# Reordering the first loads of a two-layer transformer kernel: one Wq quarter later, the second group's layernorm and transposes earlier, biases first on POOL

## Chip, cores, metric

The kernel runs on one core of one Trainium2 chip. The metric is device time in microseconds (us) of that core. Lower is better. Engines: PE (TensorE, matmul), VectorE (DVE in the profile), ScalarE (ACT), POOL (GpSimd), SP (SyncE, which here only issues DMA).

## The reference

One sequence of 2048 tokens of width 1024, in bfloat16, goes twice through two blocks: dilated local attention (32 heads, each position attends to 8 earlier positions, 2 apart) and a GELU feed-forward of width 3584.

```python
def _A_ref(x, wqkv, wo):                      # attention
    qkv = (x @ wqkv) ...                      # q, k, v: 32 heads of 32
    idx = pos[:, None] - arange(8) * 2        # masked where negative
    logits = einsum("bhsd,bhswd->bhsw", q, k[idx]) * scale
    o = einsum("bhsw,bhswd->bhsd", softmax(logits), v[idx])
    return o @ wo
x = x + _A_ref(_layernorm(x), A_wqkv, A_wo)
x = x + _B_ref(_layernorm(x), w1, b1, w2, b2)   # _B_ref: gelu(x @ w1 + b1) @ w2 + b2
# ... and both once more
```

## The kernel before

The tokens are cut into four groups of 512, four x tiles of 128 tokens each: tiles 0 to 3 are group 0, 4 to 7 group 1, 8 to 11 group 2, 12 to 15 group 3. Almost everything told here happens in the first 75 us, most of it in the stage that computes Q, K and V of group 0. Four parts matter.

The first loads, all on SP's queue:

```python
load_x(0, 0, 2)                          # x tiles 0, 1
wq_first = [load_qkv_half(0, 0, 2)]      # first half of Wq, as two quarters of 512 KB
load_x(0, 2, 4)                          # x tiles 2, 3
wq_first.append(load_qkv_half(0, 1, 2))  # second half
```

The layernorm of a tile: statistics on VectorE, the reciprocal root on POOL (two tiny operations), the normalisation on VectorE, and then a transpose, which is a DMA issued by SP for every group but the first.

```python
vec.bn_stats(...)            # twice per tile
vec.bn_aggr(mv, stats)
pool.tensor_tensor(rstd, mv[:, 1:2], eps_t, op=add)
pool.tensor_tensor(rstd, rstd, mhalf, op=pow)
vec.tensor_scalar(out=xn, in0=x[t], scalar1=mv[:, 0:1], scalar2=rstd, ...)
sp.dma_start_transpose(xnT[:, tt, :, :], xn ...)      # group 0 goes through PE instead
```

The logits, as products on VectorE (one per chunk of four channels, with an add tree over four chunks) that PE then sums over heads. A *head sum* needs four products and three adds:

```python
def new_prod(n, c):          # called after K chunk c has been copied out of PSUM
    vec.tensor_tensor(out=prod, in0=q chunk, in1=8 shifted views of the k chunk, op=mult)
    ...                      # tree: three adds per four products
def head_sum(n, last=True):  # eight matmuls on PE
    mm(L[...], lhsT=smat, rhs=prod ...)
```

And the program of the stage. PE runs its 24 chunks (8 of Q, 8 of K, 8 of V, each 8 matmuls of 128x512) in program order; `at(u, f)` calls `f` after chunk `u`. The order within VectorE, SP and ScalarE is chosen by a scheduler when the program is built; POOL keeps program order.

```python
build_constants()                         # POOL: halo zeros, masks ...
load_x(1)
stage(gen_qkv(0, 2), sides=at(0, ln_a, 1)         # layernorm of group 1 (tiles 4 to 7)
      + at(1, load_x, 3) + at(6, ln_a, 2, early)  # layernorm of group 2 (tiles 8 to 11)
      + at(14, load_bias)                         # bias load on POOL, then its transpose on PE
      + at(19, head_sum, 0, False))               # first head sum
q1 = gen_qkv(1, ...)
stage(q1, sides=at(5, attend, 0) + ...)           # attend(0): second head sum, softmax
```

Inside `gen_qkv(0)`: `load_x(2)` (tiles 8 to 11) and Wv are issued before the layernorm of group 1.

## Time and profile before

| | before |
|---|---|
| time, median of 3 runs (first measurement) | 1247.19 us (1247.05 to 1248.7) |
| span of the profiled run | 1245.8 us, granted PE clock 0.998 |
| PE busy | 1232.6 us, 99% |

From the page of the kernel before: busy time by engine, and the shares of the chain of waits that ended last.

```profile
...
PE 1232.6 (99%) x5821; PEld 633.5 (51%) x5871; DVE 835.9 (67%) x864; ACT 306.2 (25%) x477; POOL 99.1 (8%) x215
...
PE 96%; DMA 2%; DVE 1%; POOL 1%; issue 0%; SPq 0%; DVEq 0%
...
```

PE is the bound, and a share of 99% looks as if there were nothing to win. But a busy PE need not be PE at full speed: from 44 to 46 us (below) PE counts as busy for all of 2.00 us at a granted clock of 0.50, with 6 matmuls, where the same 2.00 us from 48 to 50 us hold 11 at 1.00. So we look at PE's waits. This is the wait list of PE over the whole execution (engine and line, what it waited for, us in total, number of waits, longest):

```profile
...
PE acc L179 <- DMA abc<-in_B_b_dram: 3.6, 1, 3.6
PE L L210 <- ACT xnT L93: 1.8, 1, 1.8
...
PE acc L118 <- ACT xnT L93: 0.9, 2, 0.7
```

Line L93 is the helper that issues all VectorE, ScalarE, POOL and SP instructions and L118 the one of PE's matmuls, so one reads the tile names: `acc` are PSUM accumulators, `L` the tile of the head sums (and, early on, of two transposes), `abc` first holds the biases. PE waits 3.6 us for the bias load, and 1.8 + 0.9 us in the first 18 us for copies of transposed tiles.

The wait for the biases costs more than 3.6 us. Stretches of 2 us of PE (columns: stretch; total; PE busy and number of matmuls; granted clock; share of the DMA engines; GB/s):

```profile
...
core 0: us, PE busy (x), PEclk, DMA share, GB/s
...
42.00:44.00 2.00, 1.27 (x5) 0.83 1.24 326
44.00:46.00 2.00, 2.00 (x6) 0.50 0.90 282
46.00:48.00 2.00, 2.00 (x9) 0.82 1.13 293
...
```

Behind the wait the granted clock is 0.50, and the trace has nine matmuls 427 ns apart where the others are 216 ns apart. From 46.75 us on PE has no more gap until the end.

The timeline of the stage (start, duration, engine, operation, count, and in brackets the idle time before it and what ended it). `big<-qT,kT` are products, `big<-big` adds, `L<-big,smat` is a head sum, `xn<-x` a normalisation, `rstd` POOL's part of a layernorm:

```profile
...
31.65 2.24 DVE L93 TENSOR_TENSOR big<-qT,kT 128x4096 bf16<-128x4096 bf16 x1
...
37.51 0.74 POOL L93 DMA_DIRECT2D abc<-in_B_b_dram  x1
...
42.06 0.55 DVE L93 TENSOR_SCALAR xn<-x,mv,rstd 128x1024 bf16<-128x1024 bf16 x1 [2.70 <-DMA xnT<-xn]
...
42.73 0.18 PE L179 MATMUL acc<-ident,abc 28*128 28x28 bf16 x1 [3.64 <-DMA abc<-in_B_b_dram]
...
42.85 10.54 PE L118 MATMUL acc<-xnT,wt 128*128 128x512 bf16 x40
...
47.04 4.62 DVE L93 TENSOR_TENSOR big<-big 128x4096 bf16<-128x4096 bf16 x2
...
53.32 0.61 PE L118 MATMUL L<-big,smat 128*32 128x512 bf16 x8
...
53.87 17.49 PE L118 MATMUL acc<-xnT,wt 128*128 128x512 bf16 x80
...
71.28 0.61 PE L118 MATMUL L<-big,smat 128*32 128x512 bf16 x8
...
```

Read it so. The first product starts at 31.65 us. The biases go out on POOL at 37.51, because POOL keeps program order and the last `rstd` of tiles 8 to 11 is ahead of them; they land at 42.69. PE then runs to the first head sum at 53.32. VectorE's last add before the first head sum ends at 47.04 + 4.62 = 51.66, so that sum has 1.7 us of slack and PE does not wait.

The wait for a copy in the first 18 us, in ScalarE's timeline: the copy of tile 2's transposes (`xnT<-L`) stands behind two copies of halo zeros, which wait for a POOL memset (`zhalo`) that is issued behind tile 3's `rstd`.

```profile
...
15.01 0.28 ACT L93 COPY kT<-zhalo 128x112 bf16<-128x112 bf16 x1 [5.16 <-POOL zhalo L93]
...
15.39 1.00 ACT L93 COPY xnT<-L 128x1024 bf16<-128x1024 bf16 x1
...
```

### The profile page before, as it was taken

The numbers are of one execution on the slowest core, as the hardware profiler recorded it, in microseconds if no ns is written. First come the engines' busy times: TensorE is split into PE (matmuls) and PEld (weight loads), VectorE is DVE, ScalarE is ACT, GpSimd is POOL, SyncE is SP. The second block draws the span as 40 slices with busy tenths as digits, with TensorE's granted clock in tenths as the row PEclk, the third lists the DMA queues.
The fourth block names the chain that finished last, engine by engine and source line by source line (L and its number), as shares of the span: only waits on it lengthen the run. The fifth ranks groups of instructions, "written<-read, shape, count | busy, mean of one in ns | idle before, by whom it ended". The sixth has DMA issues, their size and how long they took to land.

```text
span 1245.8 us, 14060 instructions
## 1 busy us (share of the span) xinstructions
PE 1232.6 (99%) x5821; PEld 633.5 (51%) x5871; DVE 835.9 (67%) x864; ACT 306.2 (25%) x477; POOL 99.1 (8%) x215
## 2 busy tenths in 40 slices
PE   8899999999999999999999999999999999999998
PEld 6566544456444564445644456444554444444444
DVE  6889889996995889528994379943598688012001
ACT  3333253013430135201352013510235101310310
POOL 3210112002001100101001010000000002000000
PEclk9999999999999999999999999999999999999999
DMA  9864464585745647656566565666754567546441
GB/s 298 220 206 172 136 204 151 164 207 186 199 147 203 169 138 212 180 168 156 169 184 199 165 167 173 159 198 193 198 154 148 182 203 194 165 154 196 145 140 54
DMA packets 215328, 219.83 MB, mean 176 GB/s; under 512 B 66066, under 2 KB 184992, under 8 KB 212192
## 3 DMA queue, kind: packets, MB, share of 16 engines
q1 hardware_dynamic: 212592, 208.16, 55.7%
q0 software_dynamic: 2672, 10.76, 2.7%
q8 instruction: 46, 0.75, 0.3%
q14 instruction: 18, 0.15, 0.0%
HBM read 197.40 MB, written 6.29 MB: 164 GB/s over the span
## 4 chain that ended last, share of the span: by engine, by line
PE 96%; DMA 2%; DVE 1%; POOL 1%; issue 0%; SPq 0%; DVEq 0%
PE acc L118 96%; DMA xnT<-xn 1%; POOL rstd L93 1%; DMA x<-in_A_x_dram 1%; PE L L118 0%; DMA abc<-in_B_b_dram 0%; DVE stats L93 0%; DVE xn L93 0%; SPq L93 0%; DVE mv L93 0%; PE acc L210 0%; DVE x L93 0%; PE acc L179 0%; DVEq L93 0%
## 5 line engine op out<-in xcount | busy, mean ns | idle before, releaser
L118 PE MATMUL acc<-xnT,wt 128*128 128x512 bf16 (+1 forms) x3376 | 724.4, 377 | 0.9 <-ACT xnT L93 0.9
L118 PEld LDWEIGHTS <-wt 128*128 128x128 bf16 x3376 | 398.4, 119 | 323.0 <-issue 6.7
L118 PE MATMUL acc<-wt,hT 128*128 128x512 bf16 (+1 forms) x1780 | 386.0, 376 | 2.1
L118 PEld LDWEIGHTS <-hT 128*128 128x128 bf16 x1820 | 178.1, 98 | 208.9
L93 DVE TENSOR_TENSOR big<-big 128x2048 bf16<-128x2048 bf16 (+2 forms) x182 | 239.7, 1350 | 1.6
L93 ACT ACTIVATE hT<-acc,b1T 128x512 bf16<-128x512 f32 x224 | 151.7, 687 | 318.4 <-PE acc L118 317.8
L93 DVE TENSOR_TENSOR big<-abc,vT 128x4096 bf16<-128x4096 bf16 x64 | 144.0, 2284 | 48.5 <-DMA abc<-a_d 48.4
L93 DVE TENSOR_TENSOR big<-qT,kT 128x4096 bf16<-128x4096 bf16 x64 | 143.8, 2285 | 23.7 <-ACT kT L93 23.1
L93 DVE TENSOR_TENSOR tmp<-acc,b2bc 128x512 f32<-128x512 f32 x56 | 38.7, 691 | 178.5 <-PE acc L118 174.7
L93 ACT CAST qT<-acc 128x512 bf16<-128x512 f32 x64 | 37.3, 586 | 327.3 <-PE acc L118 327.3
L118 PE MATMUL acc<-wt,oT 128*128 128x512 bf16 x440 | 97.4, 379 | 0.4
L93 DVE BATCH_NORM_STATS2 stats<-x 128x6 f32<-128x512 bf16 x128 | 84.0, 678 | 5.9 <-DMA x<-in_A_x_dram 5.0
L118 PEld LDWEIGHTS <-oT 128*128 128x128 bf16 x448 | 43.8, 98 | 52.8
L93 DVE TENSOR_TENSOR x<-acc,big 128x512 bf16<-128x512 f32 (+1 forms) x9 | 5.7, 633 | 90.0 <-PE acc L118 90.0
L93 ACT CAST vT<-acc 128x512 bf16<-128x512 f32 x64 | 37.5, 586 | 85.1 <-PE acc L118 85.1
L93 DVE TENSOR_SCALAR xn<-x,mv,rstd 128x1024 bf16<-128x1024 bf16 x60 | 32.7, 545 | 37.2 <-POOL rstd L93 32.2
L93 POOL TENSOR_TENSOR rstd<-mv,eps_t 128x1 f32<-128x1 f32 x60 | 17.0, 283 | 505.2 <-DVE mv L93 505.2
L93 ACT CAST kT<-acc 128x512 bf16<-128x512 f32 x64 | 37.5, 586 | 74.7 <-PE acc L118 74.7
L93 POOL DMA_DIRECT2D a_d<-a x32 | 19.5, 636 | 405.4 <-DVE a L93 405.4
L93 DVE TENSOR_TENSOR x<-acc,x 128x512 bf16<-128x512 f32 x64 | 43.0, 672 | 6.7 <-PE acc L118 6.4
L93 DVE TENSOR_TENSOR x<-tmp,x 128x512 bf16<-128x512 f32 x56 | 38.7, 691 | 1.7
L93 POOL TENSOR_TENSOR rstd<-rstd,mhalf 128x1 f32<-128x1 f32 x60 | 35.8, 597 | 4.7
(54 smaller groups left out, 213.1 us busy)
## 6 DMA issues: line engine op xcount, KB each, us to landing
wt<-in_B_w_dram SPq DMA_DIRECT2D x56, 1024.0 KB, 5.8
wt<-in_B_w_dram SPq DMA_DIRECT2D x64, 896.0 KB, 4.9
wt<-in_A_wqkv_dram SPq DMA_DIRECT2D x46, 1024.0 KB, 5.7
wt<-in_A_wo_dram SPq DMA_DIRECT2D x16, 1024.0 KB, 4.9
abc<-a_d POOLq DMA_DIRECT2D x32, 256.0 KB, 4.7
x<-in_A_x_dram SPq DMA_DIRECT2D x16, 256.0 KB, 7.5
out_dram<-x SPq DMA_DIRECT2D x31, 128.0 KB, 1.8
wt<-in_A_wqkv_dram SPq DMA_DIRECT2D x4, 512.0 KB, 7.8
```

The source lines that it names most:

```text
L93: inst = f(*args, **kwargs)
L118: return pe(nc.tensor.matmul(*args, **kwargs))
```

## The change

The intent: x tiles 2 and 3 land earlier if only one Wq quarter is ahead of them; the transposes of group 1 and their layernorm go ahead of the third x group and Wv; and the biases are loaded first thing on POOL after the constants, so that PE never waits for them. No work is added or removed.

```diff
+    def load_wq_piece(wt, k):
+        sp.dma_start(wt[:, k % (KD // 2):k % (KD // 2) + 2, :], wqkv_v[:, k:k + 2, 0:D])
     load_x(0, 0, 2)
-    wq_first = [load_qkv_half(0, 0, 2)]
+    wq_first = [wpool.tile([P, KD // 2, D], BF16, name="wt") for _ in range(2)]
+    load_wq_piece(wq_first[0], 0)
     load_x(0, 2, 4)
-    wq_first.append(load_qkv_half(0, 1, 2))
+    for k in range(2, KD, 2):
+        load_wq_piece(wq_first[k // (KD // 2)], k)
 ...
+    b1_rows = attp.tile([KF, P], BF16, name="abc")
     def load_bias():
-        b1_rows = attp.tile([KF, P], BF16, name="abc")
         pool.dma_start(b1_rows[:], B_b1.rearrange("(j p) -> j p", p=P))
         pool.dma_start(b2bc[:], B_b2.unsqueeze(0).to_broadcast([P, D]))
+    def transpose_bias():
         ps = psum.tile([P, KF], BF16, name="acc", bufs=6)
         pe(nc.tensor.transpose(ps[:], b1_rows[:], ident[:KF, :KF]))
 ...
         if n == 0:
+            ln_a(1)
             load_x(2)
             wv = load_qkv(2)
 ...
-                if (kq, c) in ((2, 3), (3, 1)):
+                if (kq, c) in ((1, 5), (2, 5)):       # PE's transposes of tiles 2 and 3
                     transpose_on_pe(*first_late.pop(0))
 ...
     build_constants()
+    load_bias()
     with tc.tile_pool(name="early", bufs=1) as early:
         load_x(1)
-        stage(gen_qkv(0, 2), sides=at(0, ln_a, 1) + at(1, load_x, 3) + at(6, ln_a, 2, early)
-              + at(14, load_bias) + at(19, head_sum, 0, False))
+        stage(gen_qkv(0, 2), sides=at(6, ln_a, 2, early) + at(7, load_x, 3)
+              + at(14, transpose_bias) + at(19, head_sum, 0, False))
```

More of the change, by code (lines that the diff above doesn't have):

```diff
@@ L125, in load_x @@
             sp.dma_start(x[t][:], x_in[t * P:(t + 1) * P, :])
-    def load_qkv_half(which, h, pieces=1):
-        wt = wpool.tile([P, KD // 2, D], BF16, name="wt")
-        n = KD // 2 // pieces
-        for i in range(pieces):
-            k = h * (KD // 2) + i * n
-            sp.dma_start(wt[:, i * n:(i + 1) * n, :], wqkv_v[:, k:k + n, which * D:(which + 1) * D])
-        return wt
-    def load_qkv(which):
-        return [load_qkv_half(which, h) for h in range(2)]
+    def load_qkv(which):
+        tiles = []
+        for h in range(2):
+            wt = wpool.tile([P, KD // 2, D], BF16, name="wt")
+            sp.dma_start(wt[:], wqkv_v[:, h * (KD // 2):(h + 1) * (KD // 2), which * D:(which + 1) * D])
+            tiles.append(wt)
+        return tiles
+    def load_wq_piece(wt, k):
+        sp.dma_start(wt[:, k % (KD // 2):k % (KD // 2) + 2, :], wqkv_v[:, k:k + 2, 0:D])
     load_x(0, 0, 2)
-    wq_first = [load_qkv_half(0, 0, 2)]
+    wq_first = [wpool.tile([P, KD // 2, D], BF16, name="wt") for _ in range(2)]
+    load_wq_piece(wq_first[0], 0)
     load_x(0, 2, 4)
-    wq_first.append(load_qkv_half(0, 1, 2))
+    for k in range(2, KD, 2):
+        load_wq_piece(wq_first[k // (KD // 2)], k)
     warm = bigp.tile([P, P], BF16, name="big")
```

## The prediction

> **What bounds it now.** TensorE. The page gives PE busy 1232.6 of 1245.8 us; the chain of waits is 96% PE. After 46.75 us the PE timeline has no gap worth naming. Before it PE loses:
> - about 2.0 us at 14.7 to 18.2 us: the transposes of x tile 3 wait for ScalarE's copy of tile 2 (1.8 us in the wait list), then 0.2 us;
> - 3.6 us at 39.1 to 42.7 us: the bias transpose waits for the bias load, issued by POOL at 37.5 us and landed at 42.69;
> - about 1.9 us after that: nine matmuls start 427 ns apart instead of 216 (the windows give a granted clock of 0.50 at 44 to 46 us). [...]
>
> Together 7.5 us.
>
> **What the change does.** It adds and removes no work.
> 1. One Wq quarter (512 KB, 1.34 us of DMA by the landings, which follow issue order) moves behind x tiles 2 and 3. Tile 2 lands near 8.7 us instead of 10.07; its layernorm (3.0 us), the halo copies and the transposes follow: PE wins about 1.3 us.
> 2. The biases are issued near 15 to 16.5 us and land long before 38 us: 3.6 + 1.9 us vanish there.
> 3. DMA transposes of tiles 4 to 7 go ahead of x tiles 8 to 11 and Wv. Wv should land near 36, before PE needs it (40).
>
> **How much reaches the end.** Without a new wait PE would reach the first head sum (53.32 us now) near 46.6. But that sum needs four products and three adds of VectorE, which end at 51.66 us now: a slack of only 1.7 us. In the VectorE order of the changed kernel the first product still stands after the statistics of tiles 8 to 11, and those tiles come later: transpose 4 lands about 1 us behind Wk (23 us), 5 and 6 by 25.3, tile 8 near 26.5 (now 22.9), the others to about 30. From tile 8's statistics to the first product is about 8.5 us of VectorE and rstd work, so the first product starts near 35 us instead of 31.65. It then runs with less waiting (the 2.7 us wait for a transpose at 39.4 us goes): about 17.3 us to the last add, so 52.3 (an estimate). PE then waits about 5 to 6 us at the head sum in place of the bias, and pays the slow clock again, about 2 us. The net is about 0.
>
> **Predicted:** 1247.0 us, 1243.0 to 1249.8. Faster by over 2%: 0.5%; within 2%: 99%; slower: 0.5%.
>
> **What would show it.** Tile 2 lands near 8.7; the 128x512 matmuls of the first K chunks start about 1.3 us earlier; no PE wait for the biases; a PE wait of 4 to 6 us on the products at the head sum, near 46 to 52 us, with matmuls 427 ns apart behind it; first product at 34 to 36 us; tile 8 landing at 26 to 27.
>
> **What would make it wrong.** If transposes 4 to 6 are issued without delay and tile 8 lands by 23 us, VectorE starts its products near 30 and most of 6.8 us is kept: about 1241. If transpose 8 (behind Wv) lands after 40 us, VectorE stalls before its first add and the kernel comes out at 1250 or more.

The sum: 2.0 + 3.6 + 1.9 = 7.5 us. "The slow clock again, about 2 us" is the author's estimate, the 1.9 us of the trace before carried over to another wait.

## The result, and the profile after

| | before | after |
|---|---|---|
| median, runs of one session | 1247.12 us (1246.94 to 1248.7, 4 runs) | 1248.36 us (1247.85 to 1248.87, 4 runs) |
| ratio | | 1.0007, 95% interval 0.999 to 1.0024 |
| span of the profiled run | 1245.8 us | 1247.2 us |

A ratio here is the mean time of one kernel's runs over that of the other's of the same rounds, so it is not quite the ratio of the medians that are quoted.

PE's busy time on the page after:

```profile
...
PE 1235.8 (99%) x5871; PEld 633.7 (51%) x5871; DVE 836.1 (67%) x864; ACT 306.2 (25%) x477; POOL 97.6 (8%) x215
...
```

It rose by 3.2 us (1235.8 against 1232.6) with the same share of 99%, and no matmul was added: part of it is matmuls at half clock (2.37 us behind the wait after, 1.7 before, both worked out here), and some records missing before may be in it. The wait list of PE after:

```profile
...
PE L L118 <- DVE big L93: 6.2, 1, 6.2
...
PE L L215 <- ACT xnT L93: 0.3, 1, 0.3
```

The wait for the biases is gone and the wait for the copy fell from 1.8 to 0.3 us. In their place stands one wait of 6.2 us, for VectorE's sums, at the first head sum. The stretches around it:

```profile
...
core 0: us, PE busy (x), PEclk, DMA share, GB/s
...
50.00:52.00 2.00, 0.00 (x0) 0.60 1.05 394
52.00:54.00 2.00, 1.76 (x10) 0.50 0.83 304
54.00:56.00 2.00, 2.00 (x6) 0.50 0.03 11
56.00:58.00 2.00, 2.00 (x8) 0.70 0.00 0
58.00:60.00 2.00, 2.00 (x11) 1.00 0.00 0
...
```

The clock falls to 0.50 as before, and stays there longer: the clock record has it low from 50.39 to 57.21 us, twice the 3.41 us of before, and PE works in 4.97 us of that. The timeline after, the lines that answer to those of before:

```profile
...
26.61 1.29 DVE L93 BATCH_NORM_STATS2 stats<-x 128x6 f32<-128x512 bf16 x2 [2.76 <-DMA x<-in_A_x_dram]
...
35.12 2.28 DVE L93 TENSOR_TENSOR big<-qT,kT 128x4096 bf16<-128x4096 bf16 x1
...
37.08 0.18 PE L184 MATMUL acc<-ident,abc 28*128 28x28 bf16 x1
...
37.60 2.12 POOL L93 TENSOR_TENSOR rstd<-mv,eps_t 128x1 f32<-128x1 f32 x1 [3.58 <-DVE mv L93]
...
40.39 0.55 DVE L93 TENSOR_SCALAR xn<-x,mv,rstd 128x1024 bf16<-128x1024 bf16 x1 [0.71 <-POOL rstd L93]
...
47.57 4.62 DVE L93 TENSOR_TENSOR big<-big 128x4096 bf16<-128x4096 bf16 x2
...
52.24 1.05 PE L118 MATMUL L<-big,smat 128*32 128x512 bf16 x8 [6.20 <-DVE big L93]
...
53.22 19.42 PE L118 MATMUL acc<-xnT,wt 128*128 128x512 bf16 x80
...
72.57 0.62 PE L118 MATMUL L<-big,smat 128*32 128x512 bf16 x8
...
```

The biases are there when PE comes for them at 37.08 us; it stood at that place at 42.73 - 3.64 = 39.09 before, so PE is 2.0 us ahead of its old schedule when it meets the old stall, and 5.7 us ahead behind it. But the last add on VectorE ends at 47.57 + 4.62 = 52.19 us, 0.5 us later than before. Tile 8's statistics start only at 26.61, when the tile has landed, and the first product at 35.12 instead of 31.65.

The POOL line at 37.60 us shows a smaller cost on the same path. An addition on 128x1 elements took 2.12 us beside a VectorE product and ended when the product did (39.72 against 39.67 us); at 33.20 us, with no product beside it, it took 0.19. The kernel before shows the same: 2.12 us at 31.81, beside the product that runs from 31.65 to 33.89. What the two engines contend for is not shown. The normalisation behind it waited 0.71 us at 40.39. ScalarE's copy is earlier, still behind the halo copies:

```profile
...
13.01 0.29 ACT L93 COPY kT<-zhalo 128x112 bf16<-128x112 bf16 x1 [3.00 <-POOL zhalo L93]
...
13.38 1.00 ACT L93 COPY xnT<-L 128x1024 bf16<-128x1024 bf16 x1
...
```

The account of the whole difference, read from the timelines of PE:

| PE, us | before | after | difference |
|---|---|---|---|
| first head sum starts | 53.32 | 52.24 | -1.08 |
| from there to the second head sum (8 + 80 matmuls) | 17.96 | 20.33 | +2.37 |
| second head sum starts | 71.28 | 72.57 | +1.29 |
| span | 1245.8 | 1247.2 | +1.4 |

PE stood ready for the head sum at 52.24 - 6.20 = 46.04 us, 7.28 us earlier than before. The wait took 6.20 of these, and the slow clock behind it another 2.37 (nine gaps of 427 ns between matmuls, and a head sum of 1.05 instead of 0.61 us): 7.28 - 6.20 - 2.37 = -1.29. Of that, 0.7 us is only that the low clock cost 2.37 us here and 1.7 behind the bias wait before. A loss of 1.3 us is within the scatter of the runs; the large parts of opposite sign are not.

### The profile page after: what moved, and what is told of

Same layout as the page of the kernel before. It is cut to its first block, busy times and chain, and to the rows that moved or that the text cites. A ratio compares the mean times of both kernels' runs of the same rounds, so it can differ in the third digit from the quotient of the medians.

```text
span 1247.2 us, 14104 instructions
## 1 busy us (share of the span) xinstructions
PE 1235.8 (99%) x5871; PEld 633.7 (51%) x5871; DVE 836.1 (67%) x864; ACT 306.2 (25%) x477; POOL 97.6 (8%) x215
## 4 chain that ended last, share of the span: by engine, by line
PE 96%; DVE 1%; POOL 0%; issue 0%
PE acc L118 95%; DVE big L93 1%; PE L L118 1%; POOL rstd L93 0%; DVE xn L93 0%; PE acc L215 0%; DVE stats L93 0%; DVE x L93 0%; DVE mv L93 0%
```

## The experiments

Theory A: behind the bias stall, VectorE's products are the next limit, and the first head sum cannot start before about 52 us whatever PE does. Rival B: the biases and the Wq quarter are worth their 7 us, and only the reordering of the transposes and the third x group spoils it by putting the products late. All kernels gave correct results. "Before" in each row is the kernel before in the same session; five rounds each.

| run | what differs | median us | ratio to before, 95% | PE's wait at the first head sum | last add before it ends |
|---|---|---|---|---|---|
| e1_bias | before + early biases | 1247.87 | 1.0003 (0.999 to 1.0015) | 4.5 us | 52.55 |
| e2_wq | before + Wq quarter | 1246.27 | 0.9995 (0.9982 to 1.0009) | none (biases: 4.0) | 49.71 |
| e3_ln1 | before + reordering | 1248.13 | 1.0006 (0.9994 to 1.0019) | none (biases: 5.4) | 51.95 |
| e4_wq_bias | after without reordering | 1247.65 | 1.0000 (0.9987 to 1.0012) | 5.9 us | 52.07 |
| e5_hold15 | after, layernorm of 8 to 11 behind all products | 1240.53 | 0.9949 (0.9936 to 0.9962) | none | 43.12 |
| e6_before_hold15 | before, with that hold | 1241.69 | 0.9958 (0.9947 to 0.997) | none | 44.63 |
| e7_sum_late | after, head sum four chunks later | 1246.88 | 0.9998 (0.9986 to 1.0011) | none (second: 4.5) | 52.41 |
| e8_fill | after, 24 useless matmuls in the wait | 1246.27 | 0.9995 (0.9983 to 1.0006) | 0.8 us | 52.47 |
| e9_no_reorder_hold | e4 with the hold | 1240.74 | 0.9947 (0.9934 to 0.9959) | none | 44.47 |
| e10_hold11 | after, layernorm between the two halves of the products | 1247.74 | 1.0003 (0.9989 to 1.0016) | none (second: 4.4) | 43.52 |
| e11_zhalo | e6 + halo memset early | 1240.90 | 0.9951 (0.9939 to 0.9964) | none | 44.81 |
| e12_both | e5 + halo memset early | 1239.79 | 0.9939 (0.9927 to 0.9952) | none | 42.93 |

The last column is start plus duration of the last pair of adds in VectorE's timeline.

### One part at a time: e1_bias, e2_wq, e3_ln1, e4_wq_bias

Edits of e1_bias (on the kernel before); e2_wq is the Wq part of the diff above with the two moved transposes; e3_ln1 the `ln_a(1)` part; e4_wq_bias is e1 and e2 together.

```diff
     build_constants()
+    load_bias()
 ...
-              + at(14, load_bias) + at(19, head_sum, 0, False))
+              + at(14, transpose_bias) + at(19, head_sum, 0, False))
```

> The kernel before with the early bias load alone. Theory A (behind the bias stall the next limit is VectorE's four products and three adds for the first head sum, which end at 51.7 us in the kernel before, whatever PE does): the bias wait of 3.6 us is gone, PE reaches the head sum near 47.8 us and waits there about 3.5 to 4 us with matmuls 427 ns apart behind it; 1246 to 1248 us, that is within 1.3 us of the kernel before. Rival B (the early biases are worth their 3.6 us of wait and 1.9 us of slow clock, and only the reordering of transposes and third x group spoils it in the changed kernel): no wait above 1 us at the head sum, 1241 to 1242.5 us.

Measured: no bias wait, a wait of 4.5 us at the head sum (3.5 to 4 were expected), 1247.87 us. Removing the largest visible stall of the kernel, 3.6 us and a slow clock, gave nothing. Theory A holds and rival B falls for the biases: no reordering is in this kernel.

> The kernel before with the Wq quarter behind x tiles 2 and 3 and the two moved transposes, nothing else. Theory A: x tile 2 lands 1.3 us earlier or more, PE runs 1 to 2 us ahead until the bias transpose and waits that much longer for the biases, which still come behind the last rstd of tiles 8 to 11; 1246.5 to 1248 us. Rival (PE time won at the start is kept): 1245.5 us or less.

Measured: tile 2 lands at 8.02 us (10.07 before), PE waits 4.0 us for the biases, 1246.27 us. The time is just below the expected range and not to be told from the kernel before (the interval holds 1). Its profiled run was 1.8 us faster than that of before, with the head sum at 51.42: there the biases happened to land 2.7 us after their issue, against 5.2 us before. What the Wq quarter is worth by itself is thus not measured well by this run; that PE's lead ends in the bias wait is. VectorE in this run, to which point 4 at the end comes back (tile 8 landed at 21.59 us):

```profile
...
29.98 4.44 DVE L93 TENSOR_TENSOR big<-qT,kT 128x4096 bf16<-128x4096 bf16 x2
...
45.09 4.62 DVE L93 TENSOR_TENSOR big<-big 128x4096 bf16<-128x4096 bf16 x2
...
```

> The kernel before with the layernorm and transposes of tiles 4 to 7 ahead of tiles 8 to 11 and Wv, nothing else. Theory A: tile 8 lands near 26 to 27 us instead of 22.9, the first product starts near 35 instead of 31.65, the last rstd of tiles 8 to 11 comes near 40 to 41 and the bias load behind it lands near 45 to 46, so PE waits for the biases about 6 us instead of 3.6 and the head sum comes near 55 to 56 instead of 53.3; 1249 to 1250.5 us. Rival (the reordering is harmless by itself): 1247 us.

Measured: first product at 34.70 us, tile 8 landing at 26.18, bias load issued at 39.88 and landed at 44.10, PE waits 5.4 us, head sum at 55.40; 1248.13 us. The steps are as expected but for the bias load, which took 4.2 us instead of about 5, and the median is 0.9 us under the expected range. The interval holds 1, so a loss by the reordering alone is not shown by time; the span of the profiled run is 2.1 us longer, which is the 2.1 us that the head sum is later.

> The changed kernel without its reordering: Wq quarter and early biases, transposes of tiles 4 to 7 where they were. Theory A: PE reaches the head sum near 46 us, the last add of VectorE ends near 50 to 51.5, PE waits 4 to 5 us and pays about 2 us of slow clock: 1245.5 to 1247.5 us. Rival B (only the reordering spoils the change): no such wait, 1240 to 1241.5 us.

Measured: 1247.65 us, just above the range of theory A and far from that of rival B. The timeline of this kernel, which has no reordering:

```profile
...
32.32 4.44 DVE L93 TENSOR_TENSOR big<-qT,kT 128x4096 bf16<-128x4096 bf16 x2
...
42.47 0.55 DVE L93 TENSOR_SCALAR xn<-x,mv,rstd 128x1024 bf16<-128x1024 bf16 x1 [1.07 <-DMA xnT<-xn]
...
47.45 4.62 DVE L93 TENSOR_TENSOR big<-big 128x4096 bf16<-128x4096 bf16 x2
...
52.13 1.04 PE L118 MATMUL L<-big,smat 128*32 128x512 bf16 x8 [5.92 <-DVE big L93]
...
```

The first product starts at 32.32 us here, 2.8 us earlier than after the change, but two normalisations among the products wait for DMA transposes, 1.36 us at 38.59 and 1.07 us at 42.47, and the last add ends at 52.07 us all the same. The reordering only moves VectorE's waiting from between the products to in front of them. Rival B has fallen, and with it one sentence of the prediction (see below).

### Moving the layernorm of tiles 8 to 11: e5_hold15, e9_no_reorder_hold, e6_before_hold15

If the products are late because the layernorm of group 2, which nobody needs before the stage after next, stands among them, then holding it behind them must free the head sum. `hold` makes everything on VectorE that is issued from then on follow the last product's add. Merely calling `ln_a(2)` later does not do it: in a build of that (not run), the scheduler still puts the layernorm of three of the four tiles ahead of the first product.

```diff
-        stage(gen_qkv(0, 2), sides=at(6, ln_a, 2, early) + at(7, load_x, 3)
+        stage(gen_qkv(0, 2), sides=at(7, load_x, 3) + at(15, hold) + at(15, ln_a, 2, early)
               + at(14, transpose_bias) + at(19, head_sum, 0, False))
```

> The changed kernel with the layernorm of tiles 8 to 11 held behind all eight products on VectorE. Theory A (the order on VectorE puts the products late, and that is what eats the gain): the first product starts near 27.5 us, as soon as the first K chunk is copied; the third add ends near 43.5, ahead of PE, which reaches the head sum near 46 and does not wait; no slow clock behind it; the second head sum comes near 64 us instead of 72.6. 1239 to 1241 us. Rival (the work of VectorE as such is too much in this stage, so the wait returns later, at the second head sum, at the softmax or at the output projection): 1244 us or more, with a PE wait of over 2 us elsewhere before 140 us.

Measured: 1240.53 us, as theory A expects. VectorE and PE in this kernel:

```profile
...
27.17 6.70 DVE L93 TENSOR_TENSOR big<-qT,kT 128x4096 bf16<-128x4096 bf16 x3 [4.09 <-ACT kT L93]
...
38.50 4.62 DVE L93 TENSOR_TENSOR big<-big 128x4096 bf16<-128x4096 bf16 x2
...
45.70 0.61 PE L118 MATMUL L<-big,smat 128*32 128x512 bf16 x8
...
46.25 17.49 PE L118 MATMUL acc<-xnT,wt 128*128 128x512 bf16 x80
...
54.35 4.62 DVE L93 TENSOR_TENSOR big<-big 128x4096 bf16<-128x4096 bf16 x2
...
63.67 0.61 PE L118 MATMUL L<-big,smat 128*32 128x512 bf16 x8
...
```

The first product starts at 27.17 us, as soon as the K chunk has been copied, the last add of the first half ends at 43.12, and PE runs through both head sums. The second sum is at 63.67 us, 7.6 us earlier than before; the span is 7.3 us shorter. The layernorm of group 2 now fills the time in which VectorE used to wait for the second head sum (4.68 us before), and some more: the softmax behind that sum starts at 68.24 us, about 4 us earlier than before (72.19), where PE is 7.6 us earlier. The rival (the work comes back later as another wait) falls, but not by much: VectorE finishes the input of the first output projection 0.6 us ahead of PE (126.12 against 126.69 us), where it had 4.2 us in the kernel before (130.06 against 134.31).

> Wq quarter, early biases and the hold of tiles 8 to 11 behind all eight products, but with the third x group and Wv ahead of the transposes of tiles 4 to 7 again. Theory A (refined by the run without the reordering, which waits 5.9 us as well: not the place of tile 8's load but the layernorm of tiles 8 to 11 among the products makes the head sum late): the reordering is worth nothing either way, no PE wait at the head sum, 1239.8 to 1241.3 us, as with it (1240.5). Rival (the hold needs transposes 4 to 7 early): 1243 us or more, with the first product later than 30 us.

Measured: 1240.74 us without the reordering, 1240.53 with it in the session before. The reordering is worth nothing that these runs show, either way.

> The kernel before with only that hold: layernorm of tiles 8 to 11 behind all eight products. POOL then has no rstd of tiles 8 to 11 in front of the bias load, so the biases go out near 22 to 24 us by themselves. Theory A: no bias wait, no wait at the head sum (reached near 47.8 us), 1241 to 1242.5 us, so this one line is worth four times the Wq quarter. Rival (the three moves of the change are needed to gain): 1245 us or more.

Measured: 1241.69 us. The biases go out at 22.49 us without being moved, because POOL no longer has the `rstd` of group 2 in front of them. One line on the kernel before is worth 5.3 us (1247.03 in that session against 1241.69); the three moves of the change on top of it about 1.2 us (1241.69 against 1240.53 in the same session). Of these the early biases can hardly be it, since PE has no bias wait here.

### Where the wait goes if it is only pushed: e7_sum_late, e10_hold11

```diff
-              + at(14, transpose_bias) + at(19, head_sum, 0, False))
+              + at(14, transpose_bias) + at(23, head_sum, 0, False))
```

> The changed kernel with the first head sum four V chunks later in PE's order (6.9 us of matmuls ahead of it), nothing moved on VectorE. Theory A: PE reaches the head sum near 53 us, just behind the last add (52.2), so no wait there; the second head sum, reached near 64 to 65, then waits for VectorE's eighth product, which ends near 68, about 3 to 4 us; 1243 to 1245.5 us. Rival (the wait at the head sum is not VectorE's products but the PSUM tile or the order of the queue): the wait stays about 6 us and the time 1248 us.

Measured (edit on the changed kernel): 1246.88 us. The first head sum does not wait, the second one does, by 4.5 us, and the clock falls behind it:

```profile
...
68.45 1.04 PE L118 MATMUL L<-big,smat 128*32 128x512 bf16 x8 [4.51 <-DVE big L93]
...
```

The place of the wait was as expected, its length and the slow clock behind it larger, so the time is 1.4 us above the expected range. The rival falls.

```diff
-        stage(gen_qkv(0, 2), sides=at(6, ln_a, 2, early) + at(7, load_x, 3)
+        stage(gen_qkv(0, 2), sides=at(7, load_x, 3) + at(11, hold) + at(11, ln_a, 2, early)
```

> The changed kernel with the layernorm of tiles 8 to 11 held behind the first four products only, so it stands between the two halves of the products. Theory A: the first head sum is free (last add near 43.5 us), but the second half of the products is put back by 8 to 9 us of layernorm work, its last add ends near 67.5 to 69, PE reaches the second head sum near 64 and waits 4 to 5 us with a slow clock behind it: 1245.5 to 1247.5 us. Rival (only the first head sum is tight): 1240 to 1241.5 us.

Measured: 1247.74 us, again with a wait of 4.4 us at the second head sum; the last add there ends at 63.85 + 4.62 = 68.47 us.

```profile
...
68.52 1.04 PE L118 MATMUL L<-big,smat 128*32 128x512 bf16 x8 [4.37 <-DVE big L93]
...
```

PE worked at the low clock for 6.1 us here, longer than estimated; the median is 0.2 us above the range. From the first product to the second head sum VectorE has eight products and six adds, about 32 us (27.17 to 58.97 us in e5_hold15). There is room for the layernorm in front or in between only if PE waits for it.

### The slow clock by itself: e8_fill

```diff
+    def fill(count):
+        ps = acc_tile()
+        for _ in range(count):
+            mm(ps[:], lhsT=ident[:], rhs=ident[:].unsqueeze(1).to_broadcast([P, NTT, P]), start=True, stop=True)
 ...
-              + at(19, head_sum, 0, False))
+              + at(19, fill, 24) + at(19, head_sum, 0, False))
```

> The changed kernel with 24 useless 128x512 matmuls (5.2 us) in front of the first head sum, inside the wait of 6.2 us. They add no wait to the head sum and keep PE busy. Theory A: the head sum still starts near 52.2 us, but the matmuls behind it start 216 ns apart at once, and the kernel wins the slow-clock part alone, about 2.3 us (ten matmuls 427 ns apart and a head sum of 1.05 instead of 0.61 us): 1245.5 to 1246.5 us. Rival (the slow stretch is not due to PE's idling, but to the wait's end, such as DMA traffic): still 427 ns apart, 1248 us or more.

Measured: 1246.27 us, in the range.

```profile
...
46.41 5.34 PE L118 MATMUL acc<-ident 128*128 128x512 bf16 x24
52.52 0.61 PE L118 MATMUL L<-big,smat 128*32 128x512 bf16 x8 [0.77 <-DVE big L93]
53.07 17.49 PE L118 MATMUL acc<-xnT,wt 128*128 128x512 bf16 x80
70.49 0.61 PE L118 MATMUL L<-big,smat 128*32 128x512 bf16 x8
...
```

The head sum starts at 52.52 us, no earlier than after the change, but it takes 0.61 us and the 80 matmuls behind it take 17.49 us, as in the kernel before. The span is 2.1 us shorter than after the change (by the runs' times alone, 1246.27 is not to be told from the kernel before). So the wait of 6.2 us gives back the lead, and the idling costs about 2 us on top. In the traces here the clock fell at every wait of 3.6 to 6.2 us and at none of 1.8 us or less; waits in between did not occur. This run shows a cure as well: 24 useless matmuls (5.34 us) inside the wait left one of 0.77 us, and a mean granted clock of 1.000 instead of 0.997.

### The last small wait: e11_zhalo, e12_both

```diff
     def build_constants():
-        pool.memset(zhalo[:], 0.0)
 ...
     warm_up(16)
+    pool.memset(zhalo[:], 0.0)
     ln_first()
```

> The kernel before with the hold behind all eight products, and POOL's memset of the halo zeros moved ahead of the first group's rstd work. If ScalarE's copy of tile 2's transposes really waits for that memset and not for the transposes or for tile 2's load, the PE wait of 1.5 us on that copy falls under 0.6 us, PE gains about 1 us, and the kernel comes to 1240.2 to 1241.2 us (1241.7 without). If it waits for something else: the wait stays 1.5 us, 1241.7 us.

Measured: 1240.90 us (1241.69 without, in another session). ScalarE's copy of tile 2 now starts at 13.65 us, when PE has finished its transposes, instead of behind the memset, so the memset was the cause. PE's wait for the copy is gone, but behind it came waits of 0.8 us for a normalisation and 0.5 us for POOL's `rstd`, so little of it was won; the times alone do not show a gain (1240.7 to 1243.1 us here, 1241.17 to 1242.48 without).

> The best version so far (changed kernel with the hold behind all eight products, 1240.5 us) with the memset of the halo zeros moved ahead as well. Little is left to win: the PE wait on the copy is 0.3 us there. 1239.8 to 1240.6 us, not to be told from it by time; the profile should show the wait of 0.3 us gone or halved.

Measured: 1239.79 us, all five runs between 1239.72 and 1239.87. The wait of 0.3 us on the copy is gone from the list. This version beats the kernel before, 0.9939 (0.9927 to 0.9952), and by its time the changed one too (1248.36 us, in another session). That is 0.6%, about 7.5 us: clear of noise. It is about the 7.3 us (2.0 + 3.6 + 1.7) that PE was seen to lose in the first 47 us.

## Why the prediction was right

1. **The time.** Predicted 1247.0 us (1243.0 to 1249.8), measured 1248.36: "the net is about 0" is what happened, and for the reason given: a wait at the first head sum in place of the bias wait.
2. **The steps.** Predicted and measured: tile 8 lands near 26.5 us, 26.59; first product 34 to 36 us, 35.12; last add 52.3 us, 52.19; PE's wait 5 to 6 us, 6.2; slow clock about 2 us, 2.37. The last is partly luck: over the runs the slow clock cost 1.4 to 2.8 us (see point 5).
3. **A term that was mis-sized.** "PE wins about 1.3 us" at the start: it was 2.0 us (39.09 to 37.08). Tile 2 landed at 7.90 us instead of the predicted 8.7, because the first Wq quarter landed at 7.26 instead of 8.08 us although nothing ahead of it had changed (6.71 to 8.15 us in the other runs looked at). With the wait at the head sum this had no effect on the time, as a lead of PE there has none.
4. **A statement that was wrong.** The prediction put the lateness down to the place of tiles 8 to 11 in the DMA order: "those tiles come later", and if tile 8 landed by 23 us "most of 6.8 us is kept: about 1241". The run without the reordering shows otherwise: its first product comes 2.8 us earlier, and it waits 5.9 us and takes 1247.65 us. Tile 8 landed at 24.01 us there, so the condition of that sentence was missed by a microsecond; e2_wq meets it, with tile 8 at 21.59 and the first product at 29.98 us, and its last add still ends at 49.71. PE without a bias wait would have been there near 46 us (an estimate: it stood at the biases at 41.12 - 4.02 = 37.10 us, and needs 9.0 us from there in the changed kernel), so at most 3.6 of the 6.8 us could have been kept, before any slow clock. What failed in that sentence is the term of 17.3 us from first product to last add, carried over to early loads: 17.07 after the change, but 19.73 in e2_wq and 19.75 in e4_wq_bias, where the waits for transposes fall among the products. What makes the head sum late is that the layernorm of tiles 8 to 11 stands among the products on VectorE at all; shown by the runs that hold it behind them (1240.53 with the reordering, 1240.74 without).
5. **The scatter, and what stays open.** Runs with a long wait in them scatter more: the kernel before ranged from 1244.3 to 1249.8 us over all sessions, e12_both by 0.15 us. The record shows what goes with it. In every trace with a long wait the clock was low once before the kernel's last microseconds, for 3.41 us (before, e1_bias, e2_wq) or 6.83 us (after, e3_ln1, e4_wq_bias, e7_sum_late, e10_hold11), and what that cost depends on how much of it PE spent working: 1.4 us in e4_wq_bias to 2.8 us in e10_hold11, read as PE's time from the end of the wait to its first matmul of the output projection, less that of e5_hold15. Of the 29 runs of the kernel before with a clock on record in the experiments' sessions, the three with a mean of 1.000 took 1244.3 to 1245.3 us, the nineteen with 0.998 or 0.999 1246.3 to 1248.2, the seven with 0.997 1247.4 to 1249.8. What decides which it is was not tested; transfers that land at different times (the biases took 2.7 to 5.2 us when loaded late) may do it.

## What to carry to other kernels

Before removing the largest wait of the bounding engine, look how much slack the next wait on its path has: here it was 1.7 us behind a stall of 3.6 us and a slow clock of 1.7, and three moves that won PE 7 us of lead won nothing. Then look what stands in front of the work that is waited for: a layernorm needed over 40 us later stood among products needed now, and holding it back was worth more than all the moves together, even freeing the biases by itself. Waits of the matmul engine of 3.6 to 6.2 us cost 1.4 to 2.8 us more each through its clock here, so a wait that was merely pushed to another place was paid for again (4.5 us in e7_sum_late and 4.4 us in e10_hold11, each with the slow clock behind it).

## Also measured: the clock's return, and transposing DMAs

- From the first instruction behind a wait to the clock's return it took 3.0 us (e4_wq_bias, 52.13 to 55.09), 4.0 us (before, 42.73 to 46.71), 5.0 us (after, 52.24 to 57.21) and 6.1 us (e10_hold11, 68.52 to 74.64). At the low clock the matmuls of these runs were 427 ns apart, otherwise 216.
- Two queued transposes of 256 KB landed 0.85 us apart (28.50 and 29.35 us before), copies of 256 KB 0.67 us apart, so the transposes took about a quarter longer here (other loads were under way, so this is not a test of the bandwidth).
- A transpose held SP's queue for 1.24 us at least and up to 5.2 us before (the two of e4_wq_bias that start at 17.25 us held it 11.2 us together), against 0.33 to 0.9 us for a copy of 256 KB.
